# Fourier filter and gated convolution: the second forward step on 32 points instead of 64, bias as a product, back matrices loaded, and a new order

## The chip, the cores and the metric

The kernel runs on one core of a Trainium2 chip. The metric is the device time of one execution in microseconds; the number that counts is the median of several runs. A profile of one execution stands beside them.

## What is computed

There are 8 batches of 3200 positions and 256 channels. The reference, cut to what matters:

```python
X = np.fft.rfft(x, axis=1)                      # 3200 points
Yr = Xr @ w_r - Xi @ w_i + b_r
Yi = Xr @ w_i + Xi @ w_r + b_i
Yr = np.sign(Yr) * np.maximum(np.abs(Yr) - 0.01, 0.0)    # Yi likewise
y = np.fft.irfft(Yr + 1j * Yi, n=3200, axis=1)
gate = sigmoid(sum over k of conv_w[k] * y shifted by k)  # 5 taps, causal
out = (gate * (y @ w_val)) @ w_out
```

## The kernel before

**The transform in two steps.** 3200 is written as 64 x 50 (N1, N2). Step one, `p1`, takes 50-point transforms over one index: a batch comes in 8 loads of x, and for each PE makes a tile p (lines 520 in the first batch, 555 later), which is copied to a tile s1 and stored to a scratch tensor a_dram in HBM. Step two, `p2`, loads columns back as a tile a and multiplies each by a 128 x 128 matrix f2 (64 points, real and imaginary parts as rows): line 602 makes the tile s (tag ps_s2). There are 25 columns a batch; they go in pairs, u = 0 to 11, and the last one alone, u = 12 (L635, L636).

**The mix.** The tile s is split into a high part and the rest (xs, in the fp32r format of TensorE), and likewise the sum of real and imaginary parts (sx): L652 to L664. Three products by the weights follow: k_ps (L677) from the sum, y_ps (L672) from the parts, both with 128 rows and 256 columns. DVE adds k_ps and the bias into yb (L683) and then y_ps (L686). The threshold is an ACT and a DVE operation into tp (L690, L692).

**The way back.** z_ps (L715) multiplies two pairs' tp by matrices g1, in 64 x 64 quarters of the array; the result goes by z_t to z_dram in HBM. The matrices g1 are made on PE in the first batch: line 436 turns f2 by a product with the identity, and L438 scales it. Step `positions` loads zl and makes y_p (L771, quarters again) into y_sb. Then `taps` and `gated` make the convolution (acc, L825, on DVE), the gate, v_ps and o_ps (L803), and the output.

**What sets the order.** Every piece is added to a plan with an engine, a due time (`at` and an offset of the table `O`), a booked length, its inputs and the buffers that it opens. `Plan.order` then lists the pieces engine by engine: of those that could begin, the one that is due first, with a preference for keeping pieces of one tiling mode of the array together on PE ("q" quarters, "f" and "r" the whole array). The engines run their lists strictly in that order. Buffers are rings with sizes in `SLOTS`; the tiles p, z_ps, y_p, v_ps and o_ps share two PSUM tiles (ps_2), and k_ps and y_ps have one each.

**The start.** In the first batch `p1_first` makes four tile pairs p; DVE and ACT copy one each at the same time (L525), and the stores follow on the queues of SP and ACT. Between them and the first load of a, PE runs warm-up products on an idle tile (`WARM`, L916). The bias is spread over 128 rows by products of one row (L461, L463).

Of the kernel before, what the change touches and what calls it, by code (L numbers as in the profile page):

```python
# [32 lines left out]
def dft_constants():  # L33
# [7 lines left out]
    f1 = np.zeros((N2, NT, 2))
    g2 = np.zeros((NT, 2, N2))
    f2 = np.zeros((NT, 2, N1, 2, N1))
    g1 = np.zeros((NT, 2, N1, 2, N1))
    for t in range(NT - 1):
        kap = t + 1
        ph = 2 * np.pi * ((kap * n2) % N2) / N2
        f1[:, t, 0], f1[:, t, 1] = np.cos(ph), -np.sin(ph)
# [172 lines left out]
SWITCH = {"rq": 97, "fq": 97, "qr": 100, "qf": 100}  # L221
# [13 lines left out]
def act(n, kind="copy"):  # L235
# [758 lines left out]
```

## Time and profile before

| | us |
|---|---|
| median of 3 runs (880.55 to 881.28) | 881.17 |
| the profiled execution | 877.04 |
| its span in the trace | 875.3 |
| PE busy | 858.6 |
| DVE busy | 759.1 |
| ACT busy | 605.2 |

The span goes from the first to the last instruction of the program; the time holds a little more on both sides. The rows of the trace name the line of the kernel, the engine, the operation, the tile written and the tiles read, the shape and the count, then busy time, the mean of one, and the idle time ahead with what ended it. Rows of the timeline begin with the start and the length in us. PE's lengths overlap, since products are pipelined.

### The profile page before, as it was taken

Reading aid. Unit: us, or ns where it says so; the run is one execution under the profiler, and the core shown is the slowest. Engines: PE = TensorE matmul, PEld = TensorE weight load, DVE = VectorE, ACT = ScalarE, POOL = GpSimd, SP = SyncE. Lnnn points to the kernel's source line nnn. Section 1 sums busy time; section 2 is a strip of 40 time slices with the busy share of each in tenths; the row PEclk is TensorE's granted clock in tenths of the full one; section 3 lists DMA queues with packets and bytes.
Section 4 is the critical chain, followed back from the end, with each engine's and each line's share of the span. In section 5 each row is a group of like instructions: output and inputs, shape, how many; then the busy total and the mean of one; then the engine's idle time right before and its main releaser. Section 6 shows DMA issues by size and latency. Waiting matters only on the chain.

```text
span 875.3 us, 24348 instructions
## 1 busy us (share of the span) xinstructions
PE 858.6 (98%) x10372; PEld 733.5 (84%) x10372; DVE 759.1 (87%) x1139; ACT 605.2 (69%) x924; POOL 3.7 (0%) x11
## 2 busy tenths in 40 slices
PE   8899999999999999999999999999999999999997
PEld 2578887888998888988889898988889998998775
DVE  1356888999999987999689996999969999999896
ACT  1366657966877768777687766877677767776663
POOL 0000000000000000000000000000010000000000
PEclk9999999999999999999999999999999999999999
DMA  5778776655745666556673576635763454523512
GB/s 210 251 266 240 211 241 210 233 173 182 254 156 170 204 216 210 169 180 202 222 245 115 167 233 221 205 130 191 212 229 128 134 165 139 167 69 121 194 58 94
DMA packets 103464, 162.27 MB, mean 185 GB/s; under 512 B 9178, under 2 KB 77660, under 8 KB 103356
## 3 DMA queue, kind: packets, MB, share of 16 engines
q1 hardware_dynamic: 102396, 157.45, 55.6%
q10 hardware_dynamic: 960, 3.28, 1.1%
q8 instruction: 81, 1.33, 0.7%
q14 instruction: 27, 0.22, 0.1%
HBM read 82.05 MB, written 78.64 MB: 184 GB/s over the span
## 4 chain that ended last, share of the span: by engine, by line
PE 76%; DVE 16%; ACT 3%; DMA 2%; issue 1%; SPq 0%; DVEq 0%; ACTq 0%
PE y_ps L672 14%; PE v_ps L803 11%; PE o_ps L803 11%; PE s L602 9%; PE z_ps L715 8%; DVE acc L825 7%; PE k_ps L677 7%; PE y_p L771 6%; PE p L555 5%; DVE acc L867 2%; DVE gated L329 1%; PE warm L916 1%; DMA a<-a_dram 1%; PE p L520 1%; ACT acc L836 1%
## 5 line engine op out<-in xcount | busy, mean ns | idle before, releaser
L825 DVE SCALAR_TENSOR_TENSOR acc<-y_sb,cw_sb,acc 128x800 f32<-128x800 f32 (+1 forms) x264 | 262.5, 1018 | 13.1 <-ACT acc L822 12.8
L672 PE MATMUL y_ps<-w_sb,xs 128*128 128x256 f32 x1152 | 155.4, 284 | 0.4 <-DVE yb L686 0.3
L803 PE MATMUL o_ps<-gated,wo_sb 128*128 128x400 f32 x756 | 154.1, 351 | 0.1
L672 PEld LDWEIGHTS y_ps<-w_sb,xs 128*128 128x128 f32 x1152 | 143.8, 188 | 10.3 <-issue 3.1
L803 PEld LDWEIGHTS o_ps<-gated,wo_sb 128*128 128x128 f32 x756 | 134.1, 188 | 2.8 <-DVE gated L329 0.2
L803 PE MATMUL v_ps<-y_hl,wv_sb 128*128 128x400 f32 x660 | 134.1, 347 | 0.0
L803 PEld LDWEIGHTS v_ps<-y_hl,wv_sb 128*128 128x128 f32 x660 | 116.4, 188 | 0.4 <-ACT xs L656 0.4
L602 PEld LDWEIGHTS s<-f_sb,a 128*128 128x128 f32 x800 | 101.3, 191 | 16.5 <-issue 12.5
L602 PE MATMUL s<-f_sb,a 128*128 128x128 f32 x800 | 112.5, 279 | 1.9 <-ACT xs L663 1.5
L690 ACT ACTIVATE tp<-yb,nlam 128x512 f32<-128x512 f32 (+1 forms) x104 | 73.6, 708 | 56.2 <-DVE yb L686 53.6
L715 PE MATMUL z_ps<-tp,g_sb 64*64 64x256 f32 x1536 | 94.3, 381 | 0.3 <-issue 0.2
L677 PEld LDWEIGHTS k_ps<-w_sb,xs 128*128 128x128 f32 x576 | 75.8, 188 | 17.8 <-issue 9.2
L677 PE MATMUL k_ps<-w_sb,xs 128*128 128x256 f32 x576 | 88.4, 289 | 0.3 <-DVE xs L664 0.2
L683 DVE TENSOR_TENSOR yb<-k_ps,bias_sb 128x512 f32<-128x512 f32 x96 | 65.6, 684 | 18.0 <-PE k_ps L677 17.8
L692 DVE SCALAR_TENSOR_TENSOR tp<-yb,tp 128x512 f32<-128x512 f32 (+1 forms) x104 | 68.9, 663 | 13.1 <-ACT tp L690 13.1
L715 PEld LDWEIGHTS z_ps<-tp,g_sb 64*64 64x64 f32 x1536 | 55.5, 133 | 29.3 <-issue 5.2
L327 ACT CAST gated<-acc 128x800 fp32r<-128x800 f32 x63 | 54.3, 863 | 35.3 <-DVE acc L867 34.8
L836 ACT ACTIVATE acc<-acc 128x800 f32<-128x800 f32 (+1 forms) x66 | 56.2, 855 | 26.1 <-DVE acc L825 25.1
L771 PEld LDWEIGHTS y_p<-g_sb,zl 50*64 50x64 f32 x4096 | 65.6, 135 | 9.6 <-issue 2.2
L771 PE MATMUL y_p<-g_sb,zl 50*64 50x50 f32 x4096 | 70.8, 219 | 1.4 <-DVE acc L867 0.7
L686 DVE TENSOR_TENSOR yb<-y_ps,yb 128x512 f32<-128x512 f32 x96 | 65.5, 683 | 4.8 <-PE y_ps L672 4.6
L891 ACT COPY o<-o_ps 128x800 f32<-128x800 f32 x63 | 51.9, 824 | 21.2 <-PE o_ps L803 20.6
(80 smaller groups left out, 1018.3 us busy)
## 6 DMA issues: line engine op xcount, KB each, us to landing
zl<-z_dram SPq DMA_DIRECT2D x128, 200.0 KB
out<-o SPq DMA_DIRECT2D x63, 400.0 KB
a<-a_dram SPq DMA_DIRECT2D x96, 256.0 KB
z_dram<-z_t SPq DMA_DIRECT2D x48, 512.0 KB
x<-in_x SPq DMA_DIRECT2D x120, 200.0 KB
a_dram<-s SPq DMA_DIRECT2D x120, 200.0 KB
x<-in_x ACTq DMA_DIRECT2D x8, 200.0 KB
a_dram<-s ACTq DMA_DIRECT2D x8, 200.0 KB
```

The source lines that it names most:

```text
L602: nc.tensor.matmul(spec()[:, c, :, i, :], tl[ka][:, i, c * P:(c + 1) * P], f2_of(i), start=True, stop=True)
L672: nc.tensor.matmul(p[:, 1 - r, :], xm(hx, c, r), w_sb[:, m, hw, c, :], start=k == 0, stop=k == 5)
L677: nc.tensor.matmul(p, sm(hx, c), w_sb[:, 0, hw, c, :], start=k == 0, stop=k == 5)
L683: nc.vector.tensor_tensor(out=buffer(kb, "yb", [P, 2, D]), in0=tl[kk].rearrange("p (a d) -> p a d", a=1).to_broadcast([P, 2, D]), in1=bias ...
L686: add(at + 0.2, "DVE", dve(2 * D), lambda: nc.vector.tensor_tensor(out=yb(), in0=tl[ky], in1=yb(), op=ALU.add), [ky + (0,)], [kb + (0,)])
L690: nc.scalar.activation(out=buffer(kt, "tp", [P, 2, D])[:, 0:n], in_=tl[kb][:, 0:n], func=AF.Relu, bias=nlam)
L692: add(at + 0.2, "DVE", dve(n * D), lambda: nc.vector.scalar_tensor_tensor(out=tl[kt][:, 0:n], in0=tl[kb][:, 0:n], scalar=LAM, in1=tl[kt][: ...
L715: nc.tensor.matmul(p[e * HP:(e + 1) * HP, i, j * D:(j + 1) * D], g[i * HP:(i + 1) * HP, r, e * HP:(e + 1) * HP], tl[kts[j]][i * HP:(i + 1) ...
L771: nc.tensor.matmul(pv[h][e * HP:(e + 1) * HP, c, m, :], zt[half(h), m, c * P + e * HP:c * P + (e + 1) * HP], g2_sb[half(h), :], start=True ...
L803: nc.tensor.matmul(p[:, e, 0:TB], w[:, hw, c, e * P:(e + 1) * P], src(hy, c), start=n == 0, stop=n == 5)
L825: nc.vector.scalar_tensor_tensor(out=acc(c), in0=y_of(c, j), scalar=cw_sb[:, c, j:j + 1], in1=acc(c), op0=ALU.mult, op1=ALU.add)
L836: add(at + O["conv"] + 0.15, "ACT", act(nb * TB, "sigmoid"), lambda c=c: nc.scalar.activation(out=acc(c), in_=acc(c), func=AF.Sigmoid), () ...
```

## The change

**Forward on 32 points.** `p1` now takes the even and the odd 32 points apart: the matrix f1 has its own phases for the two halves h, ACT copies one half of p into s1, and DVE writes the sum and the difference of the halves into s1 (new lines 575 and 578, in the first batch 530 and 533). a_dram holds the two results one after the other. `p2` handles two pairs at once (v = 0 to 5): each column is two transforms of 32 points, 64 rows by 64 columns, and 32 such products in the four quarters of the array make the tile s for two pairs, of two PSUM banks (new line 722). The matrices f2 take half the room. The splits L652 to L664 become one operation each for two pairs. The last column keeps its untiled product.

**Bias.** A product of ones by a tile with the bias (its high and low part in rows 0 and 32, zeros elsewhere) opens each of the two sums of y_ps (new line 759), two products for the last column (691). ACT copies k_ps to a tile kc, and one DVE operation adds y_ps and kc (773). The spreading products go.

**Back matrices.** g1 is loaded in three parts (new line 441) instead of made; the identity and the turns go.

**Order and buffers.** All numbers of `O` are new, s1 goes from 3 to 2 buffers, a from 3 to 2 of double size, xs is twice as large, sx and ps_s2 fall to one (of double size), kc is new with 2; the last warm-up group grows from 11 to 14 products.

```diff
-        f1[:, t, 0], f1[:, t, 1] = np.cos(ph), -np.sin(ph)
+        for s in range(NH):
+            ph = 2 * np.pi * ((kap * (NH * n2 + s)) % (NH * N2)) / (NH * N2)
+            f1[s, :, t, 0], f1[s, :, t, 1] = np.cos(ph), -np.sin(ph)
...
-SWITCH = {"rq": 97, "fq": 97, "qr": 100, "qf": 100}
+SWITCH = {"rq": 97, "fq": 97, "qr": 170, "qf": 170}
...
-     's2': -1.722,
-     's1i': 0.898,
+     's2': -0.541,
+     's1i': -3.623,
...
-WARM = 2, 1, 1, 1, 11
-SLOTS = {"x": 3, "zl": 3, "y_hl": 2, "s1": 3, "a": 3, "xs": 2, "sx": 2, "xz": 1, "yb": 2, "tp": 3, "zst": 2,
-         "acc": 2, "g_hl": 2, "o": 2, "ps_s2": 2, "ps_y": 1, "ps_k": 1, "ps_2": 2, "a_dram": 2, "z_dram": 2}
+WARM = 2, 1, 1, 1, 14
+SLOTS = {"x": 3, "zl": 3, "y_hl": 2, "s1": 2, "a": 2, "xs": 2, "sx": 1, "xz": 1, "yb": 2, "kc": 2, "tp": 3, "zst": 2,
+         "acc": 2, "g_hl": 2, "o": 2, "ps_s2": 1, "ps_y": 1, "ps_k": 1, "ps_2": 2, "a_dram": 2, "z_dram": 2}
...
-    def make_g1(at, u):
...
-                nc.tensor.matmul(p[:, r * P:(r + 1) * P], f2_sb[:, (2 * u + r) * P:(2 * u + r + 1) * P], eye_sb, start=True, stop=True)
...
+    def load_g1(at, part):
+        t = slice(G1_PARTS[part] * 2 * P, min(G1_PARTS[part + 1] * 2, NT) * P)
+        add(at, "SP", 400, lambda: nc.sync.dma_start(out=g1_sb[:, t], in_=g1[:, t]), STORED, [("g1", part, 0)],
+            kb=(t.stop - t.start) / 2)
...
-        add(at + 0.01, "ACT", act(1024), keep, [kp + (0,)], [ks + (0,)], {ks: "s1"})
+        add(at + 0.01, "ACT", act(512), turned, [kp + (0,)], [ks + ("turned",)], {ks: "s1"})
+        add(at + 0.01, "DVE", dve(512), total, [kp + (0,), ks + ("turned",)], [ks + (0,)])
+        add(at + 0.011, "DVE", dve(512), difference, [kp + (0,), ks + ("turned",)], [ks + (1,)])
...
+    def p2(b, v, at):
+        us = (2 * v, 2 * v + 1)
...
+        def s2():
+            p = buffer(k2, "ps_s2", [P, 2, 512]).rearrange("p i (j c r h k) -> p i j c r h k", j=2, c=2, r=2, h=2)
+            for j, u in enumerate(us):
+                for h in range(NH):
+                    f = f2_sb[:, (2 * u + h) * HP:(2 * u + h + 1) * HP]
+                    for c in range(2):
+                        for i in range(2):
+                            rows = slice(i * HP, (i + 1) * HP)
+                            for e in range(2):
+                                lo = c * P + e * HP
+                                nc.tensor.matmul(p[e * HP:(e + 1) * HP, i, j, c, :, h, :], tl[ka][rows, h, j, lo:lo + HP],
+                                                 f[rows], start=True, stop=True)
...
+                    nc.tensor.matmul(p[:, 1 - r, :], ones, rows[:, (1 - r) * D:(2 - r) * D], start=True, stop=False)
...
+            add(atu + O["mix_sum"] + 0.15, "ACT", act(D), lambda kk=kk, kc=kc: nc.scalar.copy(out=buffer(kc, "kc", [P, D]), in_=tl[kk]),
+                [kk + (0,)], [kc + (0,)], {kc: "kc"})
+            add(atu + 0.2, "DVE", dve(2 * D), lambda ky=ky, kb=kb, kc=kc: nc.vector.tensor_tensor(
+                out=buffer(kb, "yb", [P, 2, D]), in0=tl[ky], in1=tl[kc].rearrange("p (a d) -> p a d", a=1).to_broadcast([P, 2, D]), op=ALU.add),
+                [ky + (0,), kc + (0,)], [kb + (0,)], {kb: "yb"})
```

**Where instructions move.** First, DVE's list at the start of the program, before (s and p are the copies and the products of `p1_first`):

```order
L910 MEMSET idle 128x512
L525 COPY s_125<-p_110 128x1024
L525 COPY s_146<-p_131 128x1024
L525 COPY s_165<-p_152 128x1024
L525 COPY s_195<-p_171 128x1024
L329 TENSOR_TENSOR w_sb<-st,w_sb 128x512
```

The same place after; s_125, s_152, s_175 and s_195 are first written by ACT:

```order
L949 MEMSET idle 128x512
L530 TENSOR_TENSOR s_130<-p_112,s_125 128x1024
L533 TENSOR_TENSOR s_125<-p_112,s_125 128x1024
L530 TENSOR_TENSOR s_156<-p_139,s_152 128x1024
L533 TENSOR_TENSOR s_152<-p_139,s_152 128x1024
L465 TENSOR_TENSOR bias_rows<-st,bias_rows 1x512
L530 TENSOR_TENSOR s_178<-p_164,s_175 128x1024
L533 TENSOR_TENSOR s_175<-p_164,s_175 128x1024
L530 TENSOR_TENSOR s_211<-p_184,s_195 128x1024
L533 TENSOR_TENSOR s_195<-p_184,s_195 128x1024
L339 TENSOR_TENSOR w_sb<-st,w_sb 128x512
```

Each copy gave way to two operations that read ACT's copy of the other half. Second, PE's list from the last warm-up group on, before (turned are the back matrices, s the forward products):

```order
L916 MATMUL warm<-idle 128x512 x11
L436 MATMUL turned<-eye_sb,f_sb 128x128 x4
L602 MATMUL s_254<-f_sb,a 128x2x64 x2
L436 MATMUL turned<-eye_sb,f_sb 128x128 x2
L602 MATMUL s_254<-f_sb,a 128x2x64 x2
L602 MATMUL s_266<-f_sb,a 128x2x64 x2
```

And after:

```order
L955 MATMUL warm<-idle 128x512 x14
L722 MATMUL s_248<-f_sb,a 64x2x32 x32
L722 MATMUL s_295<-f_sb,a 64x2x32 x32
L766 MATMUL k_ps<-w_sb,xs 128x256 x6
L565 MATMUL p_343<-x,f_sb 64x512 x4
L759 MATMUL y_ps<-bias_rows,ones 128x256
L761 MATMUL y_ps<-w_sb,xs 128x256 x6
```

The turns are gone, and the forward products of four pairs stand together ahead of the first mix. Third, PE's list in the middle of the run, before:

```order
L803 MATMUL v_ps<-y_hl,wv_sb 128x400 x12
L672 MATMUL y_ps<-w_sb,xs 128x256 x12
L677 MATMUL k_ps<-w_sb,xs 128x256 x6
L602 MATMUL s_4065<-f_sb,a 128x2x64 x4
L803 MATMUL o_ps<-gated,wo_sb 128x400 x12
L715 MATMUL z_ps<-tp,g_sb 64x256 x16
L555 MATMUL p_4119<-x,f_sb 64x512 x4
```

And after, in a stretch of the same kind:

```order
L766 MATMUL k_ps<-w_sb,xs 128x256 x6
L565 MATMUL p_5419<-x,f_sb 64x512 x4
L565 MATMUL p_5427<-x,f_sb 64x512 x4
L722 MATMUL s_5440<-f_sb,a 64x2x32 x32
L759 MATMUL y_ps<-bias_rows,ones 128x256
L761 MATMUL y_ps<-w_sb,xs 128x256 x6
```

The forward product, which stood between products on the whole array, now stands behind p in the same tiling, and serves two pairs.

More of the change, by code (lines that the diff above doesn't have):

```diff
@@ L25 @@
 Q = NH * N2
+NF = N2
 KC = 5
@@ L299, in fourier_filter_then_gated_conv @@
     wo_sb = const.tile([P, 2, 2, D], F32R, name="wo_sb")
-    bias_sb = const.tile([P, 3, D], F32, name="bias_sb")
+    ends = const.tile([P, 2, P], F32R, name="ends")
+    rows = const.tile([P, 2 * D], F32R, name="bias_rows")
+    ones = const.tile([P, P], F32R, name="ones")
     cw_sb = const.tile([P, 2, KC], F32, name="cw_sb")
@@ L464, in load_bias @@
-        add(at, "PE", 2700, spread, [("b", 0, 0), ("b", 0, 1), ("turn", "p1", 3)], [k2 + (0,), k1 + (0,)], {k2: "ps_y", k1: "ps_k"}, mode="f")
-        add(at + 0.01, "ACT", act(2 * D), lambda: nc.scalar.copy(out=bias_sb[:, 0:2], in_=tl[k2]), [k2 + (0,)], [("bias", 0, 0)])
-        add(at + 0.01, "ACT", act(D), lambda: nc.scalar.copy(out=bias_sb[:, 2], in_=tl[k1]), [k1 + (0,)], [("bias", 0, 1)])
+            nc.gpsimd.memset(f32(ones), 1.0)
+            nc.gpsimd.memset(f32(ends), 0.0)
+            nc.gpsimd.memset(f32(ends[:, 0, 0:N1 + 1]), 1.0)
@@ L468, in load_conv @@
+            nc.gpsimd.memset(f32(ends[:, 1, N1 + 1:]), 1.0)
+            nc.gpsimd.memset(f32(rows), 0.0)
+        add(-198, "POOL", 1000, marks, (), [("bias", 0, 0)])
+        add(at, "ACT", act(2 * D, "cast"), lambda: nc.scalar.copy(out=rows[0:1], in_=st()), [key + (0,)], [("bias", 0, 0)])
+        add(at + 0.01, "DVE", dve(2 * D), lambda: nc.vector.tensor_tensor(
+            out=rows[32:33], in0=st(), in1=f32(rows[0:1]), op=ALU.subtract), [key + (0,)], [("bias", 0, 0)])
     def load_conv(at):
@@ new lines, in p1 @@
+        add(at + 0.01, "ACT", act(512), turned, [kp + (0,)], [ks + ("turned",)], {ks: "s1"})
+        add(at + 0.01, "DVE", dve(512), total, [kp + (0,), ks + ("turned",)], [ks + (0,)])
+        add(at + 0.011, "DVE", dve(512), difference, [kp + (0,), ks + ("turned",)], [ks + (1,)])
+        add(at + 0.02, "SP", 1500, store, [ks + (0,), ks + (1,)], [ka + (u,)], {ka: "a_dram"} if u == 0 else None, kb=400, moves=2, ways=10)
+    HL = ((0, 0), (0, 1), (1, 0))
+    weights = lambda *names: [("w", m_, h) for m_ in names for h in ("high", "low")]
@@ L689, in relu, with threshold @@
+    stored_a = lambda b: [("a_dram", b, j if b else (j, h)) for j in range(8) for h in range(NH if b == 0 else 1)]
+    def threshold(kb, bu, at, n):
+        kt = ("tp", bu)
         def relu():
@@ L694, in p2, with back @@
             [kb + (0,)], [kt + (0,)])
+    def back(b, us, at, last=False):
+        bu = (b, us[0])
         kz, ko, kd = ("z_ps", bu), ("z_t", bu), ("z_dram", b)
-        if u % 2 == 0 and not last:
-            return
-        both = (u,) if last else (u - 1, u)
-        kts = [("tp", (b, v)) for v in both]
-        gs = [("g1", 2 * v, 0) for v in both]
+        kts = [("tp", (b, v)) for v in us]
         nz = 1 if last else 4
@@ L717, in s1i @@
                                              tl[kts[j]][i * HP:(i + 1) * HP, r, :], start=r == 0, stop=r == 1)
[L718 removed]
+        add(at + O["s1i"], "PE", 430 if last else 1776, s1i, [*[k + (0,) for k in kts], *[g1_key(v) for v in us]], [kz + (0,)],
+            {kz: "ps_2"}, mode="f" if last else "q")
         def keep():
```

414 lines of the change are left out of this document (206 added, 208 removed).

## The prediction

> **What bounds the kernel now.** I read the engines' busy shares first, then the same by stretches of time, then the instructions of TensorE (PE) in order of time, and at last the groups of VectorE (DVE) and ScalarE (ACT) with their waits.
>
> The first line of the page, and three of the stretches (from : to, length, then busy time of PE, weight loads, DVE, ACT, POOL; granted clock; DMA share and rate):
>
> ```profile
> PE 858.6 (98%) x10372; PEld 733.5 (84%) x10372; DVE 759.1 (87%) x1139; ACT 605.2 (69%) x924; POOL 3.7 (0%) x11
> ```
> ```profile
> 36.60:125.00 88.40, 86.83 (x821) 69.67 (x822) 66.36 (x141) 57.73 (x106) 0.00 (x0) 1.00 0.78 245
> ...
> 225.00:325.00 100.00, 100.00 (x1283) 89.32 (x1283) 94.37 (x140) 75.12 (x115) 0.00 (x0) 1.00 0.61 197
> ...
> 812.00:875.30 63.30, 56.01 (x705) 42.95 (x704) 50.33 (x63) 36.21 (x48) 0.00 (x0) 0.99 0.32 111
> ```
>
> PE is never idle in the middle, at a full granted clock, so work taken from PE there shortens the run one for one. DVE at 94.4 of 100 us stands close behind. In the first batch (36.6 to 125) DVE has room and PE has not. ACT, at 75, is no bound.
>
> A busy PE need not be a fast one, so I take each piece's price from the start of one piece to the start of the next. Two stretches of PE (start, length, line, tile, records; a 32-bit float product makes two records, an fp32r product one):
>
> ```profile
> 124.56 0.97 PE L677 MATMUL k_ps<-w_sb,xs 128*128 128x256 f32 x6
> 125.45 1.15 PE L771 MATMUL y_p<-g_sb,zl 50*64 50x50 f32 x64
> 126.53 1.68 PE L672 MATMUL y_ps<-w_sb,xs 128*128 128x256 f32 x12
> 128.05 0.40 PE L677 MATMUL k_ps<-w_sb,xs 128*128 128x256 f32 x2
> ```
> ```profile
> 310.80 1.91 PE L715 MATMUL z_ps<-tp,g_sb 64*64 64x256 f32 x32
> 312.53 1.06 PE L555 MATMUL p<-x,f_sb 50*64 50x512 f32 x8
> ...
> 315.76 2.35 PE L803 MATMUL o_ps<-gated,wo_sb 128*128 128x400 f32 x12
> 317.96 1.05 PE L602 MATMUL s<-f_sb,a 128*128 128x128 f32 x8
> 318.76 2.42 PE L803 MATMUL v_ps<-y_hl,wv_sb 128*128 128x400 f32 x12
> 321.02 1.57 PE L672 MATMUL y_ps<-w_sb,xs 128*128 128x256 f32 x12
> 322.43 0.86 PE L677 MATMUL k_ps<-w_sb,xs 128*128 128x256 f32 x6
> 323.12 1.05 PE L602 MATMUL s<-f_sb,a 128*128 128x128 f32 x8
> 323.94 2.42 PE L803 MATMUL o_ps<-gated,wo_sb 128*128 128x400 f32 x12
> ```
>
> Plain prices: a k_ps piece 323.12 - 322.43 = 0.69, so 0.115 a product of 256 columns; a y_ps piece 1.41. The forward product s of one pair costs 318.76 - 317.96 = 0.80, and the v_ps behind it lasts 2.26 where the o_ps ahead lasts 2.20: together 0.86, and with the pair at 323.12 (0.82 to the next start) I take 0.87.
>
> **What a change of tiling costs.** Products that use the array as four 64-wide quarters (p, z_ps, y_p) I call quarter pieces. Around the y_p piece at 125.45: it lasts 1.08, k_ps ahead of it 0.89 and y_ps behind it 1.52. The next rows give a run of two y_p pieces:
>
> ```profile
> 336.51 2.08 PE L771 MATMUL y_p<-g_sb,zl 50*64 50x50 f32 x128
> 338.52 0.71 PE L602 MATMUL s<-f_sb,a 128*128 128x128 f32 x4
> ```
>
> Two pieces take 2.01, one 1.08: a y_p piece itself is 0.93 to 0.94, and entering takes 0.14 of its own time. The y_ps behind loses 1.52 - 1.41 = 0.11; k_ps, which lies between two quarter pieces, loses 0.20 on both sides, so 0.09 on the side ahead. One run of quarter pieces costs 0.14 + 0.11 + 0.09 = 0.34 us of switching, however many pieces are in it.
>
> **The change, part by part: PE.**
>
> Forward columns. Before, 12 pairs in 8 batches make 96 pieces at 0.87: 83.5 us. After, 48 quarter pieces, each for two pairs, of 32 products with 64 columns on 64 rows. No row shows this shape. Its nearest is y_p (32 products, 50 columns, 0.94); by z_ps, 1.73 us for 32 records of 256 columns, a column costs 0.211 ns a record, so 64 columns need 64 x 64 x 0.211 = 0.86, and y_p's 50 would need 0.68. If the larger of a fixed pace (y_p's, 0.94) and the columns decides, a piece costs 0.94; if y_p's rest of 0.26 comes on top of the columns, 1.12. I take 0.94, since z_ps shows no rest beyond its columns: 45.1 us. Gain 38.4; by the other price 29.8. [...]
>
> Bias. A product of ones and the bias row ahead of each of two sums: 192 products for the pairs and 16 for the last one, 208 x 0.115 = 23.9 us lost. They lie on PE, in the full stretches; nothing hides them.
>
> Switching. The forward product was in the untiled mode, and entered from k_ps or y_ps without loss but the 0.06 counted above. In the order I count 93 runs of quarter pieces before and 103 after, since most new forward pieces lie beside a p or z_ps: 10 x 0.34 = 3.4 us lost. Were all 48 alone, it would be 16.3.
>
> Back matrices. Twelve turns of four records (half a forward piece, 0.435) leave PE in the first batch, which is full: 5.2 us gained. They come as three loads of 1.6 MB together, while the forward matrices halve; at the 0.78 share of DMA in that stretch I count no time for it, at worst the 1.6 MB at 245 GB/s, 6.5 us, and only if x waits behind it.
>
> PE together: -38.4 + 23.9 + 3.4 - 5.2 = **-16.3 us**.
>
> **DVE and ACT.** The groups (count | busy, mean ns | idle before them and its releaser), DVE, then ACT, then one row of the waits (total, times, longest):
>
> ```profile
> L683 DVE TENSOR_TENSOR yb<-k_ps,bias_sb 128x512 f32<-128x512 f32 x96 | 65.6, 684 | 18.0 <-PE k_ps L677 17.8
> ...
> L660 DVE TENSOR_TENSOR xs<-s,xs 128x512 fp32r<-128x512 f32 x96 | 65.2, 680 | 0.1
> L867 DVE TENSOR_TENSOR acc<-v_ps,acc 128x800 f32<-128x800 f32 x64 | 62.7, 982 | 2.5 <-ACT acc L836 2.3
> ...
> L659 DVE TENSOR_TENSOR sx<-s,sx 128x256 f32<-128x256 f32 x96 | 40.2, 419 | 20.0 <-ACT xs L656 18.6 <-PE turned L436 0.5
> L664 DVE TENSOR_TENSOR xs<-sx,xs 128x256 fp32r<-128x256 f32 x96 | 39.8, 415 | 0.1
> ```
> ```profile
> L560 ACT COPY s<-p 128x1024 f32<-128x1024 f32 x56 | 56.3, 1017 | 2.2 <-PE p L555 2.0
> ...
> L652 ACT COPY sx<-s 128x256 f32<-128x256 f32 x96 | 35.4, 369 | 16.4 <-PE s L602 15.2
> ...
> L465 ACT COPY bias_sb<-bias 128x512 f32<-128x512 f32 x1 | 0.6, 585 | 1.7 <-issue 1.7
> ```
> ```profile
> DVE sx L659 <- ACT xs L656: 18.6, 23, 3.9
> ```
>
> DVE loses the bias sums, 65.6 us. From 512 to 800 elements 302 ns are added, so 1024 cost about 1.22: two pairs at once take 1.22 + 0.68 + 0.68 = 2.58 where they took 2 x (0.680 + 0.419 + 0.415) = 3.03, so 48 x 0.45 = 21.6 us go. The sum and the difference behind each p piece are new: 56 x 2 x 0.684 = 76.6, and 4.9 in the first batch's own (four times 2 x 1.22 for one copy of 1.22). DVE: -5.7 in all. ACT copies half of p (585 for 1017 ns, -24.2) and k_ps (96 x 0.369 = +35.4): about even with the merged casts. Where PE is full, neither moves the end, if DVE keeps up.
>
> **The start.** Before the first pair, every p is kept by DVE and ACT side by side; now ACT copies one half and DVE then adds and subtracts, with both tiles held:
>
> ```profile
> 18.58 1.23 DVE L525 COPY s<-p 128x1024 f32<-128x1024 f32 x1 [2.04 <-PE p L520]
> ...
> 19.86 2.05 PE L520 MATMUL p<-x,f_sb 50*64 50x512 f32 x16 [0.16 <-DVE s L525]
> ...
> 21.84 1.22 DVE L525 COPY s<-p 128x1024 f32<-128x1024 f32 x1 [2.04 <-PE p L520]
> ...
> 24.67 1.01 ACT L525 COPY s<-p 128x1024 f32<-128x1024 f32 x1 [4.97 <-DMA a_dram<-s]
> ...
> 33.45 1.39 SPq L586 DMA_DIRECT2D a<-a_dram  x3
> ...
> 36.61 0.71 PE L602 MATMUL s<-f_sb,a 128*128 128x128 f32 x4
> ```
>
> The next p waits for DVE (19.86 after 18.58 + 1.23). The chain of one p is 1.22 now and 1.01 + 1.22 + 1.22 = 3.45 then, 2.23 more; four in a row end 8.9 later than 23.06, at 32.0, where before the last copy, held up by a store, ended at 25.68. So the last store leaves 6.3 later, and the load of a and the first forward product with it. SP issues the loads of w between the stores and a in both; part of the 7.8 us from 25.68 to 33.45 may be that queue, which would leave +3.5. The second forward piece then waits until the single ps_s2 tile is read, up to 1.5 more. I take **+6.0**, bounds 3.5 and 8. The three added warm products fill this wait.
>
> **New waits later.** In the order, three y_ps pieces follow another with only a k_ps (0.69) between, and two k_ps pieces adjoin. y_ps is drained by DVE:
>
> ```profile
> 322.63 0.69 DVE L686 TENSOR_TENSOR yb<-y_ps,yb 128x512 f32<-128x512 f32 x1 [0.31 <-PE y_ps L672]
> ```
>
> It begins 0.2 after y_ps ended (322.43) and lasts 0.69; with 0.2 back to PE that is 1.1, so 0.4 each. A k_ps drained by ACT at 0.37 with two such steps: 0.8 each. 3 x 0.4 + 2 x 0.8 = **+2.8**, bounds 0 and 6. s1 falls to two buffers, but p pieces lie far apart except in the first batch; load and store counts on SP stay, so I cost them at nothing, covered by two a tiles of double size.
>
> **Sum:** -16.3 + 6.0 + 2.8 = -7.5. The profiled execution has 877.04 us (span 875.3), 4.1 below the median of the runs, 881.17; the difference applies to both: 869.5 there, **873.7** as a median.
>
> **Rivals.** *The start is hidden* (stores land sooner, warm products cover): -13.5, 867.7. For it: ACT's last copy already waited 4.97 for a store. Against it: PE has nothing else to do before the first pair. Chance 0.14.
>
> *Small products cost the dearer 1.12*: 8.6 more, 882.3, about the time before. Chance 0.10. [...]
>
> *DVE becomes the bound*, slower. Its 94.4 of 100 us leaves 5.6, and PE's gain in the middle shrinks the batch while DVE's work stays. If DVE sets the pace from about 95% on, the middle's gain on PE, (38.4 - 23.9 - 3.4) x 6 / 8 = 8.3, is lost, and each of 56 new pairs of DVE operations waits for ACT as L659 does, 18.6 / 96 = 0.19 each: +10.6. Less DVE's own 5.7 x 6 / 8 = 4.3, this gives -7.5 + 8.3 + 10.6 - 4.3 = +7.1, 888.3. For it: the p tiles share two PSUM buffers with z_ps, y_p, v_ps and o_ps, and stay held through three operations for one. Against it: DVE has slightly less to do in all. Chance 0.20. [...]
>
> **Numbers.** My forecast holds 0.56 (866 to 880, by the bounds of start and waits). What a measurement can tell from no change is 0.2%, 1.8 us, so faster is under 879.4. Of the forecast 0.52 lies there, 0.04 within; with the hidden start 0.14, faster is 0.66. The dearer products halve between same and slower: same 0.09, slower 0.05 + 0.20 = 0.25. The range takes in both faster cases and the lower half of the DVE rival: 864 to 889.
>
> **What would show it.** Forward pieces of 64 records at 0.94 within a run; the ones at 0.115; the first forward product near 42.6; PE still over 99% between 225 and 725. A piece at 1.12, or a DVE at 96% with PE idle behind p or yb, would make me wrong; so would a first product before 39.

## The result, and the profile after

The changed kernel takes 915.76 us (912.23 to 917.57, four runs) against 881.22 us: a ratio of 1.0357, 95% interval 1.0307 to 1.0407. It is 34.5 us slower where I forecast 7.5 us less; my range ended at 889. A second set of four runs (after_again, below) gave 923.78, ratio 1.0442 (1.0403 to 1.0481). The profiled execution has a span of 915.8, 40.5 more than the 875.3 of before. These two profiled executions lie further apart than the medians: that of before was 4.1 us below its median, that of after 1.8 above.

First line of its page:

```profile
PE 865.2 (94%) x12830; PEld 725.1 (79%) x12830; DVE 766.7 (84%) x1008; ACT 591.9 (65%) x863; POOL 5.9 (1%) x13
```

The stretches up to the first forward product and from there on, then three stretches that the prediction used (columns as there):

```profile
0.00:46.80 46.80, 40.27 (x102) 12.08 (x102) 14.79 (x16) 8.31 (x10) 1.76 (x11) 0.78 0.57 183
46.80:915.80 869.00, 824.92 (x12728) 713.07 (x12728) 751.93 (x993) 583.54 (x853) 4.10 (x2) 0.99 0.56 178
...
36.60:125.00 88.40, 79.98 (x1074) 58.29 (x1072) 59.69 (x103) 42.40 (x71) 0.00 (x0) 0.90 0.78 233
...
225.00:325.00 100.00, 98.67 (x1530) 86.17 (x1529) 92.79 (x120) 72.00 (x104) 0.00 (x0) 1.00 0.61 197
...
425.00:525.00 100.00, 94.16 (x1541) 82.31 (x1543) 84.58 (x110) 68.03 (x99) 0.00 (x0) 1.00 0.59 185
```

The same two parts of before:

```profile
0.00:36.60 36.60, 33.02 (x116) 12.83 (x116) 6.25 (x7) 7.60 (x10) 1.15 (x9) 1.00 0.66 226
36.60:875.30 838.70, 825.55 (x10256) 720.69 (x10256) 752.88 (x1133) 597.60 (x914) 2.53 (x2) 1.00 0.57 184
```

PE was idle 13.2 us behind its first forward product and is idle 44.1 now; that product comes 10.2 us later; the granted clock, 1.00 before, is 0.78 up to it and 0.90 in the first batch. DVE's share falls: it is not what bounds the middle.

The pieces themselves, in order of time:

```profile
573.66 0.86 PE L766 MATMUL k_ps<-w_sb,xs 128*128 128x256 f32 x6
574.45 2.08 PE L812 MATMUL y_p<-g_sb,zl 50*64 50x50 f32 x128
576.35 1.12 PE L722 MATMUL s<-f_sb,a 64*64 64x64 f32 x64
577.29 0.96 PE L812 MATMUL y_p<-g_sb,zl 50*64 50x50 f32 x50
580.85 0.44 PE L812 MATMUL y_p<-g_sb,zl 50*64 50x50 f32 x14 [2.58 <-issue]
```

A forward piece (L722) of 64 records takes 577.29 - 576.35 = 0.94, as forecast. But the y_p behind it stops after 50 of its 64 records for 2.58 us, and what ended that is "issue": no semaphore, buffer or transfer of the kernel's own that the profile shows. In the waits of PE this is the first row now (total, times, longest):

```profile
PE y_p L812 <- issue: 15.7, 12, 2.6
PE y_ps L759 <- DVE yb L773: 3.9, 1, 3.9
PE s L722 <- ACT xs L749: 3.5, 1, 3.5
...
PE z_ps L626 <- DVE s L578: 1.8, 1, 1.8
```

Before, the longest row was 1.7, and the one of y_p that ends by "issue" 0.5:

```profile
PE z_ps L707 <- DVE acc L867: 1.7, 1, 1.7
...
PE y_p L771 <- issue: 0.5, 1, 0.5
```

**One account for all runs.** From the first forward product to the last piece I add up PE's records at the prices of the prediction (0.94 a forward or y_p piece, 0.117 a product of ones, 0.34 a run of quarter pieces, and so on) and call it work; what the time from piece to piece has beyond that I call waits, so a low clock counts as a wait. A stall is a stop that ends within 0.12 us of the moment 1.46 us behind the landing of a block of instructions (first experiment). Span = first product + work + waits + 7.

| run | span | first product | work | waits | of it stalls |
|---|---|---|---|---|---|
| before | 875.3 | 36.6 | 812.2 | 19.1 | 2.0 |
| after | 915.8 | 46.8 | 795.0 | 67.0 | 19.8 |
| change | +40.5 | +10.2 | -17.2 | +47.9 | +17.8 |

So the work fell by 17.2, where I forecast 16.3; the start cost 10.2 for 6.0; and the new waits 47.9 for 2.8. The work is counted at prices, so it is not a measurement by itself. What the trace shows directly is this: of the 47.9, 30.9 are more idle time of PE (44.1 for 13.2), and some 10 are half clock while PE worked. The last 7 lie in rows that the profile counts as busy.

The window for a stall turned out to be narrow. If I count PE's idle time before every stop that ends 1.15 to 1.75 us behind a landing, the stalls are 0.7 us in before, 17.1 in after and 19.5 in after_again. Below I give this wider count beside the narrow one where they differ.

### The profile page after: what moved, and what is told of

It reads as the page before. It is cut to its first block, busy times and chain, and to the rows that moved or that the text cites. A ratio compares the mean times of both kernels' runs of the same rounds, so it can differ in the third digit from the quotient of the medians.

```text
span 915.8 us, 29128 instructions
## 1 busy us (share of the span) xinstructions
PE 865.2 (94%) x12830; PEld 725.1 (79%) x12830; DVE 766.7 (84%) x1008; ACT 591.9 (65%) x863; POOL 5.9 (1%) x13
## 4 chain that ended last, share of the span: by engine, by line
PE 61%; DVE 23%; ACT 6%; issue 5%; DMA 4%; SPq 1%; ACTq 0%; DVEq 0%
PE y_ps L761 11%; PE o_ps L844 10%; PE v_ps L844 9%; DVE acc L866 8%; PE z_ps L626 6%; PE y_p L812 6%; PE k_ps L766 6%; PE p L565 4%; PE s L722 4%; DVE acc L908 3%; PE y_ps L759 2%; DVE gated L339 2%; DMA x<-in_x 2%; PE warm L955 2%; DVE yb L773 2%
## 5 line engine op out<-in xcount | busy, mean ns | idle before, releaser
L761 PE MATMUL y_ps<-w_sb,xs 128*128 128x256 f32 x1152 | 164.2, 282 | 0.0
L761 PEld LDWEIGHTS y_ps<-w_sb,xs 128*128 128x128 f32 x1152 | 151.2, 191 | 0.1
L603 ACT ACTIVATE tp<-yb,nlam 128x512 f32<-128x512 f32 x96 | 69.1, 723 | 46.3 <-DVE yb L773 45.9
L812 PE MATMUL y_p<-g_sb,zl 50*64 50x50 f32 x4096 | 76.5, 221 | 16.6 <-issue 15.7
L605 DVE SCALAR_TENSOR_TENSOR tp<-yb,tp 128x512 f32<-128x512 f32 x96 | 65.4, 684 | 13.6 <-ACT tp L603 13.6
L908 DVE TENSOR_TENSOR acc<-v_ps,acc 128x800 f32<-128x800 f32 x64 | 63.0, 984 | 15.7 <-PE v_ps L844 14.6
L773 DVE TENSOR_TENSOR yb<-y_ps,kc 128x512 f32<-128x512 f32 x96 | 65.6, 684 | 12.1 <-PE y_ps L761 11.5
L339 DVE TENSOR_TENSOR gated<-acc,gated 128x800 fp32r<-128x800 f32 x63 | 62.0, 984 | 10.1 <-ACT gated L337 10.1
L722 PEld LDWEIGHTS s<-f_sb,a 64*64 64x64 f32 x3072 | 53.5, 136 | 20.7 <-issue 12.0
L819 ACT COPY y_sb<-y_p 128x800 f32<-128x800 f32 x64 | 52.3, 825 | 22.9 <-PE y_p L812 22.7
```

The costliest lines, as they stand in the source:

```text
L339: add(at + 0.001, "DVE", dve(n), lambda: nc.vector.tensor_tensor(out=low(), in0=src(), in1=f32(high()), op=ALU.subtract), [*uses, hl[0]], ...
L603: nc.scalar.activation(out=buffer(kt, "tp", [P, 2, D])[:, 0:n], in_=tl[kb][:, 0:n], func=AF.Relu, bias=nlam)
L605: add(at + 0.2, "DVE", dve(n * D), lambda: nc.vector.scalar_tensor_tensor(out=tl[kt][:, 0:n], in0=tl[kb][:, 0:n], scalar=LAM, in1=tl[kt][: ...
L722: nc.tensor.matmul(p[e * HP:(e + 1) * HP, i, j, c, :, h, :], tl[ka][rows, h, j, lo:lo + HP], f[rows], start=True, stop=True)
L761: nc.tensor.matmul(p[:, 1 - r, :], xm(hx, j, c, r), w_sb[:, m, hw, c, :], start=False, stop=k == 5)
L773: add(atu + 0.2, "DVE", dve(2 * D), lambda ky=ky, kb=kb, kc=kc: nc.vector.tensor_tensor(out=buffer(kb, "yb", [P, 2, D]), in0=tl[ky], in1=t ...
```

## Experiments

Each ratio is against runs of the kernel before on the same chip (884.2 to 886.5 us as medians). The experiments ran on several chips. Ratios from different chips compare less surely than their intervals say: after itself came to 1.0357 and 1.0442.

**1. Where PE's instructions come from.** The row of the DMA queues that carries instructions, before and then after:

```profile
q8 instruction: 81, 1.33, 0.7%
```

```profile
q8 instruction: 101, 1.65, 0.8%
```

In both traces every packet of this row has 16384 bytes. PE's records rose from 10372 products and as many weight loads to 12830, and the packets from 81 to 101, while the instructions of DVE and ACT fell (1139 to 1008, 924 to 863). So I take the packets for PE's, each a block of about 128 products with their loads: 10372 / 81 = 128 and 12830 / 101 = 127. That is an estimate from these counts; no row says what a packet holds. The packets around the stop above, with the product records that PE began since the packet before:

```
packet starts   takes    records since the one before
   561.76       1.288      125
   569.33       1.124      113
   578.45       0.879      271
   583.45       1.151       26
   589.37       1.002      186
```

PE ran 271 records between two packets, then stood; it went on at 580.85, 1.52 us after the late packet had landed; another stop ended at 780.67, 1.47 us behind a packet of 778.32 + 0.88. Behind the first 200 us of after, PE stopped for over 0.3 us inside a y_p or forward piece 12 times, and 11 of these stops ended 1.25 to 1.55 us behind a landing. The late packet of 578.45 itself took 0.88 us, less than the others in the table, with the DMA's share at 0.52 from 574 to 578 us and 0.83 from 578 to 582. No two packets in after start closer than 3.3 us, while two y_p or forward pieces, 128 product records, take 1.9. That PE waited for the packets is my reading of this. To test it, y_p was written with the same arithmetic in half as many instructions (weights of 128 columns, no halves), once in after and once in before:

```
-   for e in range(2):
-       nc.tensor.matmul(pv[h][e*HP:(e+1)*HP, c, m, :], zt[half(h), m, c*P+e*HP:c*P+(e+1)*HP], g2_sb[half(h), :], ...)
+   nc.tensor.matmul(pv[h][:, c, m, :], zt[half(h), m, c*P:(c+1)*P], g2_sb[half(h), :], ...)
```

> The kernel after, with y_p made of 16 products of 128 weight columns a piece instead of 32 of 64 (same values, same order of pieces, half the instructions). Theory: PE's instructions come in blocks of 16 KB, 256 of them, by a DMA; in the trace of after, PE stands still inside y_p and forward pieces and goes on 1.46 us after such a block has landed, 19.8 us in all (2.0 before), since these pieces use up 256 instructions in 1.9 us. Then these stalls fall below 6 us and the blocks from 101 to about 85; the time falls by 12 to 17 us plus whatever the wider product costs or saves (up to 0.9 us a piece dearer, read from the same edit on before). Rival: y_p waits for zl or for a ps_2 tile; then the stalls inside y_p stay at 15 us or more.

> The kernel before with the same edit of y_p. It has almost no stalls of this kind, so it gives the price of the wider product: within 2 us of before if a piece costs the same 0.93 us, up to 57 us more if it costs 1.8. Theory and rival agree here.

Measured: after_wide 961.39, ratio 1.0825 (1.0771 to 1.088); before_wide 960.51, 1.0829 (1.0761 to 1.0896). The wide product is dear, and only half as many do the work; the group in before_wide:

```profile
L770 PE MATMUL y_p<-g_sb,zl 50*128 50x50 f32 x2048 | 132.5, 285 | 0.2 <-DVE acc L867 0.2
```

A piece alone takes 1.92 us from its start to the next one's, instead of 1.08, and two in a row 3.71 instead of 2.01. But the stalls are nearly gone: 1.5 us in after_wide and 1.0 in before_wide (by the wider count 1.1 and 0.0), and after_wide has 85 packets for 10782 products, again 127 each. So the stalls follow the density of instructions in these runs: 19.8 us with 64 records in the 0.93 us of a y_p piece, 1.5 with 32 in 1.79. They make 16 to 18 us of the difference between after and before.

The spans of the two wide kernels are equal, 960.7 and 960.4, but that is not the stalls alone. Behind its first product before_wide lost 35.8 us to half clock while PE worked and after_wide 20.6, where after lost 10.2 and before nothing. In before_wide most of this came while PE was never idle; one of its rows (clock 0.94):

```profile
225.00:400.00 175.00, 175.00 (x1642) 153.82 (x1642) 142.11 (x207) 114.79 (x171) 0.00 (x0) 0.94 0.55 175
```

Without the stalls, after_wide's idle time is about that of after: 20.8 us for 22.7. The stalls went, and the other waits stayed.

**2. Keeping such pieces apart.** In after_warm (experiment 4) the planner puts a y_p or forward piece off for 2.5 us behind another:

```
+ THIN, GAP = 8.0, 2500.0
- start, p = min(near, key=lambda c: (c[1]["at"] + (0.0 if e != "PE" ...
+ start, p = min(near, key=lambda c: (c[1]["at"] + (THIN if c[1].get("dense") and c[0] < thin else 0.0) + (0.0 if e != "PE" ...
```

> The kernel of the run after_warm with one more rule in the planner: a forward or y_p piece is put off while another one began less than 2.5 us before, if anything else can run. Theory of the instruction blocks: the pieces are the same, only spread, so the stalls that end 1.46 us after a block of instructions has landed fall from 13.8 us to 5 or less, and the time falls 8 to 15 us below that of after_warm. Rival, that PE waits for data and buffers in the middle: the stalls move to other pieces, and the time stays within 4 us of after_warm.

Measured: 910.09, ratio 1.0307 (1.0265 to 1.0349); after_warm had 1.0275, and 1.032 a second time. The stalls fell from 13.8 to 9.1 (by the wider count from 21.2 to 8.8) and the waits of 200 to 750 us from 30 to 10, but those from 800 on grew from 12 to 24. Its longest rows:

```profile
PE o_ps L850 <- DVE acc L914: 4.9, 3, 4.4
PE y_p L817 <- issue: 4.3, 3, 2.0
```

A better middle was paid for with a worse end. The 8 to 15 us of the theory are not shown, although the stalls went by more than half: taking them out does not by itself give their time back.

**3. Is PE still the only bound?** after_noones leaves the 192 products of ones out, so the bias of all but the last column is not added:

```
- nc.tensor.matmul(p[:, 1 - r, :], ones, rows[:, (1 - r) * D:(2 - r) * D], start=True, stop=False)
```

> The kernel after without the 192 products of ones and bias rows for the pairs (the bias of all but the last column is left out; same order of the pieces). If PE's work still sets the time, 192 x 0.117 = 22.5 us go, all of it. Rival: other waits (DVE, buffers, instruction blocks that come no sooner) fill the room; then less than 12 us go.

Measured: 912.31, ratio 1.029 (1.0228 to 1.0352). Work fell by 22.5, the waits rose from 67.0 to 84.0. Against the two measurements of after, 1.0357 and 1.0442, 6 to 13 us came out: between a quarter and 0.6 of it. DVE is not at 96% either, but at 91.08 and 84.28 of 100 us:

```profile
225.00:325.00 100.00, 95.60 (x1493) 82.35 (x1492) 91.08 (x118) 70.85 (x103) 0.00 (x0) 1.00 0.62 193
...
425.00:525.00 100.00, 92.70 (x1526) 81.30 (x1530) 84.28 (x110) 67.51 (x100) 0.00 (x0) 0.98 0.60 185
```

So no single engine is shown to bound the changed kernel; PE waits now for one, now for another. The second measurement of after, unchanged:

> The kernel after unchanged, as the yardstick for the three others on the same chip: 1.036 times the kernel before by both theories.

It had waits of 73.5, 13.6 of them stalls. The wider count gives 19.5 for after's 17.1, so the difference of 6 us from after's 19.8 comes from the narrow window: a stop of 3.22 us at 584 that ended 1.70 us behind a landing lies outside it.

**4. The start.** ACT's list in after (start, length):

```profile
10.66 1.01 ACT L526 COPY s<-p 128x1024 f32<-128x1024 f32 x1 [0.26 <-PE p L521]
...
16.27 1.53 ACTq L539 DMA_DIRECT2D a_dram<-s  x2
17.84 1.01 ACT L526 COPY s<-p 128x1024 f32<-128x1024 f32 x1 [6.17 <-DMA x<-in_x]
...
21.40 1.48 ACTq L539 DMA_DIRECT2D a_dram<-s  x2
25.15 1.01 ACT L526 COPY s<-p 128x1024 f32<-128x1024 f32 x1 [5.79 <-PE p L521]
```

ACT itself issues two stores of the difference, which DVE ends last. Its list stops there until DVE is done, and its copy of the next p stands behind these stores. So a p takes 7.2 to 7.3 us, not the 3.45 of my chain. And the clock falls, to half from 9.4 to 12.8 and from 19.6 to 36.7 us: the third p takes 3.68 us for 12 records where 16 took 2.05 in before.

```profile
21.43 3.68 PE L521 MATMUL p<-x,f_sb 50*64 50x512 f32 x12 [1.22 <-DVE s L533]
```

A smaller part is the last warm-up group, which I had put down as filling the wait. It ran at half clock until 36.7 and ended at 46.77. The first forward product began 0.06 later, though the two loads of its tile a had landed at 44.93 and 45.60. So 1 to 2 us of the late start are that group.

after_warm issues these stores on SP and puts more idle products between the pieces:

```
- WARM = 2, 1, 1, 1, 14
+ WARM = 2, 2, 3, 3, 14
- add(at + 0.02, engines[h][0], 400, lambda h=h, k=k: store(h, k), ...
+ add(at + 0.02, "SP", 400, lambda h=h, k=k: store(h, k), ...
```

> The kernel after, with the first batch's stores all on SP's queue, so that ACT's copy of the next p no longer stands behind two store issues, and 2, 3, 3 warm-up products between the p pieces instead of 1, 1, 1, so that the granted clock does not fall. Theory: the period of a p piece at the start falls from 7.2 us towards 5, the granted clock of the first 36.6 us rises from 0.72 to 0.9 or more, the first forward product comes at 40 to 43 instead of 46.8, and the time falls by 5 to 12 us. Rival: the late start is made up by slack later; then the time falls by less than 2.

> after_warm once more, as the base on the same chip for the two kernels that differ from it by one edit each: 906 to 916, ratio about 1.0275, PE's waits at about 42 us (3.5) and 95 us (3.9), the clock at 0.5 for some 6 us behind each.

Measured: 912.01, ratio 1.0275 (1.0211 to 1.0338), and 911.52, 1.032 (1.0264 to 1.0376). The p pieces run evenly, 5.4 to 5.6 apart and from the second on at full clock (2.86 to 2.89 us for 16 records, where 16 at half clock took 5.37 in after), and the first product is at 39.5 (41.1 in the second):

```profile
13.21 2.86 PE L521 MATMUL p<-x,f_sb 50*64 50x512 f32 x16
...
18.78 2.89 PE L521 MATMUL p<-x,f_sb 50*64 50x512 f32 x16
...
39.50 0.46 PE L722 MATMUL s<-f_sb,a 64*64 64x64 f32 x16
```

Of after's 10.2 us at the start, 6 to 7 are these causes; in the total 3 to 15 came out, by the pairs of ratios (1.0357 and 1.0442 against 1.0275 and 1.032).

**5. Half clock behind waits.** In after, two waits of the first batch (48 and 103 us), and the clock in the 4 us stretches with them and behind them (last columns: clock, DMA share, rate):

```profile
48.00:52.00 4.00, 0.49 (x18) 0.52 (x21) 2.41 (x3) 2.12 (x3) 0.00 (x0) 0.79 0.81 222
...
56.00:60.00 4.00, 4.00 (x22) 3.06 (x14) 2.89 (x4) 1.02 (x2) 0.00 (x0) 0.50 0.91 245
104.00:108.00 4.00, 0.64 (x3) 0.64 (x4) 3.86 (x8) 1.26 (x3) 0.00 (x0) 0.62 0.88 273
108.00:112.00 4.00, 4.00 (x21) 4.00 (x21) 3.04 (x7) 1.21 (x4) 0.00 (x0) 0.53 1.03 227
```

Summed over the stretches from 46.8 on, length times what the clock is short of 1.00, the loss comes to some 13 us in after, 10 of them while PE worked; before lost under 1. In these rows half clock began within the waits of 3.5 and 3.9 us and lasted 10.2 and 6.8 us. In other rows of after it does not go by the length of the stop: half clock of 3.4 us also followed the shorter stops of 1.54 us (to 591.74) and 2.37 (to 780.67), and none followed the one of 2.58 (to 580.85):

```profile
578.00:582.00 4.00, 1.42 (x32) 1.23 (x25) 1.59 (x2) 1.45 (x3) 0.00 (x0) 1.00 0.83 213
...
590.00:594.00 4.00, 2.46 (x35) 2.28 (x27) 3.96 (x6) 2.70 (x5) 0.00 (x0) 0.88 0.54 192
...
782.00:786.00 4.00, 4.00 (x76) 3.72 (x74) 1.82 (x2) 2.62 (x5) 0.00 (x0) 0.72 0.35 113
```

And before_wide fell to half clock with no wait at all: 0.94 over 175 us in which PE was busy throughout (experiment 1). What sets the clock is thus not shown here. after_fill lets PE run eight idle products in the first of the two long waits:

```
+ if b == v == 0:
+     pf = buffer(("fill", 0), "ps_k", [P, D])
+     for _ in range(8):
+         nc.tensor.matmul(pf, tl[ki][:, 0:P], tl[ki][:, 0:D], start=True, stop=True)
```

> after_warm with eight idle products of 256 columns (0.43 us each, 3.4 in all) on PE between the first and the second forward piece, where it waits 3.5 us for the single ps_s2; the order of all else is as it was. Nothing is left out. Theory A, a wait of this length lowers the granted clock for what follows: the clock stays at 1.00 from 44 to 52, where it was 0.50 and 0.78, and the pieces behind come out about 3 us earlier, though not one microsecond of waiting was removed: 3 us of the total, ratio about 1.024. Rival, the low clock there comes from something else (the work itself, or the start): the clock stays as it was and the time is equal to after_warm's within 1 us.

The stretches in after_warm_2, then in after_fill:

```profile
44.00:48.00 4.00, 0.97 (x36) 1.00 (x40) 2.42 (x3) 1.69 (x3) 0.00 (x0) 0.53 0.89 222
48.00:52.00 4.00, 4.00 (x56) 2.72 (x49) 1.39 (x2) 2.54 (x5) 0.00 (x0) 0.62 0.85 250
52.00:60.00 8.00, 8.00 (x120) 6.18 (x119) 6.17 (x10) 3.14 (x6) 0.00 (x0) 1.00 0.82 246
```

```profile
44.00:48.00 4.00, 3.94 (x80) 3.16 (x78) 2.32 (x3) 1.51 (x3) 0.00 (x0) 1.00 0.81 224
48.00:52.00 4.00, 3.23 (x12) 1.28 (x13) 2.58 (x4) 2.09 (x4) 0.00 (x0) 0.79 0.86 228
52.00:60.00 8.00, 8.00 (x115) 6.31 (x115) 4.67 (x8) 2.14 (x5) 0.00 (x0) 0.89 0.77 243
```

The clock stayed up from 44 to 48 and fell later and less: 1.7 us short in these 16 us instead of 3.4. The total did not move: 913.17, ratio 1.0323 (1.0275 to 1.037), against 1.032. So the idle products held the clock up while they ran, as theory A had it, but half clock came from 50.3 to 53.7 all the same, with no stop over 0.9 us ahead of it. What was saved here did not come out at the end, and 2 us cannot be told in runs that spread by 4.

**6. The block of steps on DVE.** The wait at 95 to 99 us in after_warm, on DVE (13 steps that unpack w_val) and then on PE:

```profile
91.69 2.13 DVE L378 TENSOR_SCALAR st<-st 128x512 int32<-128x512 int32 x5
...
98.37 0.68 DVE L773 TENSOR_TENSOR yb<-y_ps,kc 128x512 f32<-128x512 f32 x1
```

```profile
99.11 0.58 PE L759 MATMUL y_ps<-bias_rows,ones 128*128 128x256 f32 x1 [3.88 <-DVE yb L773]
```

The new table put this block ahead of yb. after_later takes after_thin and puts its due time back; after_spread takes after_warm and sets one step behind each following DVE operation, all else in its order:

```
-  'later': -19.515,
+  'later': 21.111,
```

```
+ for p in rest:
+     done.append(p)
+     if moved and (p["engine"] == "DVE" or moved[0]["engine"] == "ACT"):
+         done.append(moved.pop(0))
```

> after_thin with one due time put back to the one of before: the steps that unpack w_val and w_out from 64-bit words on DVE come 40 pairs' times later (later: -19.515 to 21.111). Nothing is left out. Theory A, that these 13 steps ahead of yb and s on DVE's list make the waits of 3.88 us at 103 and 1.78 at 139: these two go, and the time falls from 910 by about 4 to 6, to 904 to 906, ratio 1.024 to 1.027. Rival: the whole table is fitted together and the steps only stand in another's way, nearer to the tail: the two waits go but as much comes back elsewhere, 908 to 920.

> after_warm with the 13 unpacking steps of w_val, and of w_out, no longer in one block on DVE's list: one step behind each following DVE operation, the order of all else kept on every engine. Nothing is left out. Theory A: the block of 7 us stands ahead of yb and of s and makes PE's waits of 3.9 us at 95 and 2.6 us at 130; spread, each becomes under 1 us, and the clock behind the first stays at 1.00: 3 + 2 + about 4 of clock, so some 7 to 9 us, ratio about 1.018. Rival: DVE has no room there at all, and the same time is waited in small pieces: under 3 us.

Measured: after_later 929.59, ratio 1.049 (1.0445 to 1.0534), 1.8 points above its base: for its waits of 3.9 and 2.8 at 96 and 131 us there are 2.2 at 107 and 3.5 at 116. The waits of 4.2 and 4.4 near the end (873 and 900) are not new: the base has 3.8 and 4.4 at 855 and 882. What came on top lies mostly between 200 and 750 us, where PE is idle for 15 us instead of 4; the stalls rose from 9.1 to 12.0 (by the wider count from 8.8 to 14.3). after_spread 915.66, 1.0349 (1.0292 to 1.0406), no gain over after_warm's 1.032. The waits of its first batch:

```profile
PE z_ps L639 <- DVE tp L618: 4.1, 1, 4.1
...
PE k_ps L779 <- ACT kc L784: 3.5, 3, 2.5
```

The wait behind yb fell to 1.3, and one of 4.1 came for z_ps, 9 us later. My theory fell: moving the block moves the wait and does not remove it. Where the wait stands, DVE is full in both runs, from 90 to 100 us in after_warm_2 and from 100 to 110 in after_spread:

```profile
90.00:100.00 10.00, 7.10 (x74) 5.03 (x70) 9.62 (x19) 3.31 (x6) 0.00 (x0) 0.94 0.69 189
```

```profile
100.00:110.00 10.00, 5.10 (x50) 3.63 (x48) 9.47 (x31) 2.77 (x6) 0.00 (x0) 0.94 0.83 247
```

That DVE has no room at all, as the rival had it, is not shown: from 90 to 100 us in after_spread it is busy for 7.37 of 10.

**7. The order.** after_oldO is after with the due times of before; before_g1 is before with only the back matrices loaded, its table kept:

```
-  O = {'hold': 7.808, 'together': 3.726, 'later': -19.515, ...
+  O = {'hold': 0.867, 'together': 110.825, 'later': 21.111, ...
```

> The kernel after, with the table of due times of before; pieces, buffers and instructions as after. Forward and y_p pieces lie less in a row there (by counting in the two orders I expect about a third of the stalls: 5 to 9 us instead of 19.8). Theory of the instruction blocks: these stalls fall by 10 to 15 us; the time is 5 to 15 us below after if the old table costs nothing elsewhere. Rival, that the loss is in the pieces themselves: within 5 us of after.

> The kernel before with one part of the change alone: the back matrices loaded in three parts, no turns and no identity. PE loses 24 products of 0.22 us in the first batch, which is full: 3 to 6 us less than before. Rival, that the 1.6 MB of loads delay x and a in a stretch whose DMA share is 0.78: no gain or up to 5 us more.

Measured: after_oldO 969.65, ratio 1.0958 (1.0899 to 1.1018), waits 125.9; before_g1 901.17, 1.0192 (1.0152 to 1.0231): its work fell by 3.4, its waits rose from 19.1 to 43.7. Both theories of after_oldO missed, as did the gain that I forecast for before_g1. The largest row of waits of each:

```profile
PE y_ps L759 <- DVE yb L773: 16.0, 12, 3.9
```

```profile
PE s L595 <- DMA a<-a_dram: 5.1, 3, 3.5
```

Taking 3.4 us of work out of before made it 17 us slower. The order was not fitted to it, but the edit also adds the 1.6 MB of loads, and its largest waits are for a, as the rival had it: the longest, 3.5 us, stands just ahead of the first product (at 38.0 instead of 36.6), with half clock from 36.9 to 43.8. Most of the other waits are for results of DVE and ACT. How much belongs to the loads and how much to the order is not separated. I then sought a table anew: for after_warm and, alike, for before, with a rule that 128 instructions of a y_p or forward piece must be in a stock that fills at 52 per us (a rate set for the planner; by my estimate, two blocks of 254 that start 3.3 us apart, the closest in after, would give 77):

```
+ STOCK, SUPPLY = 240.0, 0.052
+ could = [(max(c[0], stocked + max(0.0, 128 - stock) / SUPPLY), c[1]) if c[1].get("dense") else c for c in could]
-  O = {... 'load_z': -4.723, ... 'project': 6.914, ... 'later': -19.515, ...
+  O = {... 'load_z': 3.677, ... 'project': 18.718, ... 'later': -46.138, ...
```

> The changed kernel with the first batch's stores all on SP's queue and the longer warm products (as in after_warm), its planner told that a y_p or forward piece takes 128 instructions, of which 240 are in stock and 52 come in a us (other work takes 17 a us), and its table of due times sought anew under that rule. Nothing is left out. Theory A, the new waits belong to the order and to the instructions' supply, not to the change: work stays 795, the first forward product at about 39.5, the instruction stalls fall from 13.8 to under 5 and the other waits from 57 to about 30: span 875 to 885, ratio 0.993 to 1.01. Theory B, the waits belong to the changed pieces themselves (one ps_s2, a p held through three operations): the waits stay at 60 or more and are only moved: 900 to 912, ratio 1.02 to 1.035.

> The kernel before with the same rule for instructions (for its 64 y_p pieces) and its table sought anew in the same way, for about as long; its start is left as it is. Nothing is left out. Theory A: it has 19 us of waits in all, 2.0 of them stalls for instructions, so at most some 10 us can come out; a search over the order gives 0.99 to 1.0. If it gains as much as after_fit against after_warm, what after_fit gains says nothing of the change. Theory B says the same here: 0.99 to 1.0.

> after_fit with both edits, the idle products behind the first forward piece and the spread unpacking. Nothing is left out. Theory A: its waits of 3.5 us at 41, 4.3 at 95 and 2.7 at 131, with the clock's share, shrink by 10 to 13 us: 890 to 893 for its 902.65, ratio 1.007 to 1.010, still slower than before, since 9 us of stalls and the tail remain. Rival: what goes there comes back behind DVE: 898 to 902.

Measured: after_fit 902.65, ratio 1.0214 (1.0187 to 1.0241): 9 us under after_warm by the medians, 0.6 to 1.1 points by the ratios; stalls 9.2 (by the wider count 12.5 for after_warm's 21.2). Theory A's 875 to 885 did not come; the time and the waits, 904.4 - 39.1 - 795.0 - 7 = 63.3, lie where theory B put them. before_fit 892.88, 1.0111 (1.0086 to 1.0137), outside both forecasts: the same search made before 9 us slower, so it does not find orders as good as the one that before had, and theory B is not shown by after_fit either. after_fit2, with the edits of 5 and 6 as well, 907.74, 1.024 (1.0189 to 1.029), no gain: its profiled execution has a span of 895.3 and waits of 52.1, but its runs reach from 897 to 910. No version beat before. Between the two kernels with orders sought in one way, 1.0 point of the 3.6 is left, with after's start mended. But before_fit's start became worse, with the first product at 41.7 instead of 36.6. From the first products on, the medians differ by (902.65 - 39.1) - (892.88 - 41.7) = 12.4 us, 1.4 points.

## Why the prediction was wrong, point by point

- **Work on PE, -16.3: the prices were right.** A forward piece is 0.94, not 1.12; ones take 324.90 - 324.79 = 0.11; the merged DVE operations have the forecast lengths (1.217, 0.685 and 0.681 us). The account's -17.2 is counted at these prices. PE's busy time behind the first product, with half clock taken out, fell by 0.6 + 10.2 = 10.8; what the other 6 are is not shown. The rival of dearer small products is out: 64 records in 0.94 us are 14.7 ns each. What the many small products cost came in another place, in the stalls: 19.8 us where before had 2.0 (third point).

```profile
324.79 0.28 PE L759 MATMUL y_ps<-bias_rows,ones 128*128 128x256 f32 x1
324.90 0.86 PE L761 MATMUL y_ps<-w_sb,xs 128*128 128x256 f32 x6
```

- **Start, +6.0 (3.5 to 8): mis-sized, +10.2.** I chained ACT, DVE, DVE and left out that ACT issues stores of DVE's last result ahead of its next copy, and that the clock is at half under p and under the warm-up products. Both are removed in after_warm. The longer warm-up group, which I had as filling the wait, held the first product up by 1 to 2 us.
- **"New waits later", +2.8 (0 to 6): the step that failed, +47.9.** I counted three y_ps and two k_ps pieces that stand too close, each for its buffer. Shown in its place: 17.8 us of stalls for instructions (16.4 by PE's idle time alone), a cause that I had not on my list though before's one row of 0.5 us had it; 10 to 12 us of half clock, 7 to 8.5 of them with the two long waits of the first batch; and some 18 for buffers and results. From its first product to 200 us PE stands still for 13.1 us, where it stood 3.2 before. For the last part, the experiments show that the waits move and do not go: with the table (7), with the unpacking steps (6), with the stalls (2). Why they are there stays open.
- **PE over 99% from 225 to 725: wrong**, 94 to 99% by the stretches shown. "Work taken from PE there shortens the run one for one" did not hold in the changed kernel: in after_noones 6 to 13 us of 22.5 came out.
- **DVE as the bound** was my slow rival, 888.3: right in sign, 27 us short, wrong in place. DVE is under 93 of 100 in the stretches of the middle; it is full for some 10 us in the first batch, with PE idle behind it.
- **Not settled:** what share of the last 18 us belongs to the change itself (one ps_s2, p held through three operations) and what to an order that could be mended. The difference of after_fit and before_fit, 1.0 point, holds both, and the start of each. A second ps_s2 tile was not tried. Nor is it shown what sets the granted clock.

## What to carry to other kernels

When an edit makes many small instructions of few large ones, count instructions per microsecond over a few microseconds, not only their durations (here 12830 products for 10372, and 19.8 us of stalls for 2.0): look at the packets of the instruction queue, and at waits that end by "issue" inside a run of one kind. A busy share of 98% in an order that was fitted to the kernel is no spare capacity that an edit can draw on: the old table under the changed pieces cost 54 us (969.65 for 915.76), and a small edit that took 3.4 us of work out, and added loads, cost 17. Price a change by its work, its start and the waits of the new order apart, and give the last the range that a changed order has shown. When two kernels come out equal, look at the granted clock of both before crediting an edit.

## What the runs showed of the hardware that I had not expected

- The row q8 instruction has packets of 16384 bytes: 81 in before and 101 in after, about 128 products with their loads a packet by my estimate from the counts. In after, 11 of 12 stops inside a y_p or forward piece behind 200 us ended 1.25 to 1.55 us behind a landing, and no two packets started closer than 3.3 us. Of four such pieces of 64 records each, one behind another, the last stopped for 2.58 us, with 271 product records between two packets.
- In after the granted clock was at half in spells of 3.4 us or a multiple of it (3.4, 17.1, 10.2, 6.8, 3.4 and 3.4, and one that the end cut). Those of 10.2 and 6.8 us began within waits of 3.5 and 3.9, and 3.4 us followed stops of 1.54 and 2.37, but none followed one of 2.58. In before_wide half clock came while PE was busy for 175 of 175 us (0.94). I had not counted it: some 13 us behind after's first product, and p pieces at half speed ahead of it.
- 50-row products of 50 columns (before and before_wide): a second piece in a row adds 0.93 us with 64 weight columns (64 records, 14.5 ns each) and 1.79 us with 128 (32 records, 56 ns each).
